# One turning transfer for the two chunks of a group, and a new order of loads and preparations, in a retention-and-mixer kernel

## The chip, the cores and the metric

The kernel runs on 1 core of one Trainium2 chip. The metric is the time of one execution in microseconds on the device; the profile is of one such execution. The engines of the core are named as in the profile: PE is TensorE (PEld its weight loads), DVE VectorE, ACT ScalarE, POOL GpSimd, SP SyncE. All loads from memory and all turning transfers (DMAs that transpose 16-bit data within the on-chip memory) are issued by SP, in the order of its queue; weights and most results go out by POOL's queue.

## The reference

```python
# q, k, v: (8 batches, 8 heads, 576 rows, 64), float32
scores = scale * q @ k.T                      # per batch and head
Dmat   = gamma[h] ** (i - j) for i >= j, else 0
x      = ((scores * Dmat) @ v)  -> (batch, 576, 512)      # heads side by side
h      = x.T @ U @ V                          # U: (576, 32), V: (32, 576)
u      = x + h.T
out    = u + max(u @ w_ch1, 0) @ w_ch2        # w_ch1: (512, 2048), w_ch2: (2048, 512)
```

## The kernel before

**Tiling.** Two batches lie one behind the other as 1152 rows, cut into nine chunks of 128 rows (`NI = 9`); the fifth chunk of a pair (`J = 4`) holds the last 64 rows of one batch and the first 64 of the next, so that it is loaded in halves. The first pair of batches is worked on by a front that is written out by hand (`front`, L937 to L1182). The three other pairs are the stream: 27 chunks, numbered 0 to 26 here, where chunk n is `order[NI + n]`.

**One streamed chunk.** `load` (L245) issues on SP the DMAs of k, q and v into three float32 tiles of the pool `stage` (15 tiles; L257). `prep` (L616) then does three things: `cast_qk` (L262) makes bf16 of k (L271, on VectorE for the first chunks, on POOL from chunk 5 on) and of q (L273, on ACT); `scale_v` (L277) makes bf16 of v times a decay (L282, POOL); `xbar` (L287) issues on SP one turning transfer of the chunk's q and k, 128x1024 elements (L290). The turned tile `qkT` feeds the scores, the bf16 k and v the states.

**Groups.** The stream is worked on in groups of one or two chunks: 0 | 1,2 | 3,4 | 5 | 6,7 | 8, and then twice (two, two, one, two, two): 9,10 | 11,12 | 13 | 14,15 | 16,17 and so on (L1194). Four steps belong to a group: W swaps halves of v (`swap_v`, L364, VectorE); S is `section` (L428): the output products of the group before (L401, L412), the scores of this one (L321, which need `qkT`), its state products (L338), and on VectorE the scaling of the outputs (L420) and the running states (L371, L373); C casts the states on ACT (L380); M multiplies the scores by the mask on VectorE (L351).

**The body.** For each batch b from 1 to 7 (L1233) a list of large products is the main work: `Y1` (L545), u times w_ch1 into one of three PSUM buffers (L553), evicted with a maximum on ACT (L559); `Y2` (L583), the result times w_ch2 (L588), to which VectorE adds u (L577) and which POOL stores (L580). Into this list `merge` (L16) puts the other steps, each at a share of the list's estimated cost that is written out by hand: `fills` (L1223) has W, S, C and M and the mixer's steps, `places` (L1215) the shares at which chunks are loaded and prepared. The mixer of the next batch (`mixer_items`, L441) makes u: two small products (L457, L493), an addition on VectorE (L499), and the turning of u on SP (L511), four chunks in one transfer of 128x2048 for an even batch, three and two chunks for an odd one. Each engine runs its instructions in the order in which they are written out so, and SP too: a transfer that waits for a cast holds back every load behind it.

Of the kernel before, what the change touches and what calls it, by code (L numbers as in the profile page):

```python
# [10 lines left out]
BF16 = mybir.dt.bfloat16  # L11
# [25 lines left out]
def kernel(  # L37
# [11 lines left out]
    nc = tc.nc  # L49

    B, H, S, D = q.shape
    dm = H * D
    dff = moe_w_ch1.shape[1]
    R = moe_U.shape[1]
    P = 128
    HALF = 64
    NHP = H // 2
    NF = dff // P
    NCC = dm // P
    NI = 9  # L60
# [7 lines left out]
    def pool(name, bufs, **kw):  # L68
        return ctx.enter_context(tc.tile_pool(name=name, bufs=bufs, **kw))

    consts = pool("consts", 1)
    stage = pool("stage", 15)
    qk_pool = pool("qk_pool", 9)
    v_pool = pool("v_pool", 9)
    qkT_pool = pool("qkT_pool", 9)
    ret_pool = pool("ret_pool", 5)
    s_pool = pool("s_pool", 2)
    x_pool = pool("x_pool", 1)
# [162 lines left out]
        return [(slice(0, HALF), e, J * P), (slice(HALF, P), e + 1, 0)]  # L241

    ch = {}

    def load(pr, i, which, seg=None, gate=False):  # L245
        c = ch.setdefault((pr, i), {})
# [15 lines left out]
    def cast_qk(pr, i, rows=slice(0, P), eng=None, k_eng=None, js=(1, 0)):  # L262
        c = ch[pr, i]
        if "qk" not in c:
            c["qk"] = qk_pool.tile([P, 2, dm], BF16, tag="qk", name="qk")
        t = c["qk"]
        if eng is not None:
            for j in js:
                copy(eng, t[rows, j, :], c["f", j][rows].rearrange("p h d -> p (h d)"))
            return  # L270
        (k_eng or nc.vector).tensor_copy(  # L271
            out=t[rows, 1, :], in_=c["f", 1][rows].rearrange("p h d -> p (h d)"))
        nc.scalar.activation(  # L273
            out=t[rows, 0, :], in_=c["f", 0][rows].rearrange("p h d -> p (h d)"),
            func=AF.Copy)
# [9 lines left out]
        )  # L285

    def xbar(pr, i):  # L287
        c = ch[pr, i]
        c["qkT"] = qkT_pool.tile([P, 2 * NHP, P], BF16, tag="qkT", name="qkT")
        nc.sync.dma_start_transpose(  # L290
            out=c["qkT"], in_=c["qk"].rearrange("p j n -> p (j n)")
        )

    st = {}

# [318 lines left out]
    order = [(pr, i) for pr in range(B // 2) for i in range(NI)]  # L614

    def prep(g):  # L616
        pr, i = order[g]
        cast_qk(pr, i, k_eng=nc.gpsimd if g >= NI + 5 else None)
        scale_v(pr, i)
        xbar(pr, i)  # L620

    un = [dict() for _ in range(4)]
    def unit_i0(u):
        return 2 * u + (1 if u >= 2 else 0)

    def unit_views(u, j, hh):
        if j not in un[u]:
            un[u][j] = qk_pool.tile([P, 2, dm], BF16, tag="qk", name="qk")
        w = slice(hh * 4 * D, (hh + 1) * 4 * D)
        return (un[u][j][:, :, w].rearrange("p j (h d) -> p h j d", d=D),  # L630
                un[u]["f", j, hh].rearrange("p (h j) d -> p h j d", j=2))
# [24 lines left out]
    def T_cp(u, j, eng, hps=slice(0, NHP)):  # L656
        pst = un[u]["pst", j]
        if ("T", j) not in un[u]:
            un[u]["T", j] = qkT_pool.tile([P, 2 * NHP, P], BF16, tag="qkT", name="qkT")
        t = un[u]["T", j]  # L660
        if j == 1:
            copy(eng, t, pst)
            return

        copy(eng, t.rearrange("p a b -> p (a b)").rearrange(
            "p (hp t j) -> p j hp t", hp=NHP, j=2)[:, :, hps],
            pst.rearrange("p (j hp) t -> p j hp t", j=2)[:, :, hps])
# [110 lines left out]
    def cast_J(r, eng, js):  # L778
        c = ch[0, J]
        if "qk" not in c:  # L780
            c["qk"] = qk_pool.tile([P, 2, dm], BF16, tag="qk", name="qk")
        for j in js:
            copy(eng, c["qk"][r, j, :].rearrange("p (t h d) -> p h t d", t=2, d=D),
                 c["f", j][r].rearrange("p (h t) d -> p h t d", t=2))
# [11 lines left out]
    def T_J(r, engs, k_at=None, q_at=None):  # L796
        c = ch[0, J]
        pst = {}
        for j, (pool_, tag) in ((1, k_at or (ps_big, "big")), (0, q_at or (ps_big, "big"))):
            pst[j] = pool_.tile([P, NHP, P], BF16, tag=tag, name="pst")  # L800
            for x in range(2):
                for t in range(2):
                    nc.tensor.transpose(  # L803
                        pst[j][:, 2 * x + t, r], c["qk"][r, j, (2 * t + x) * P:(2 * t + x + 1) * P],
                        ident[r, r])
        if "qkT" not in c:
            c["qkT"] = qkT_pool.tile([P, 2 * NHP, P], BF16, tag="qkT", name="qkT")
            c["kT"] = kTJ
        copy(engs[0], c["kT"][:, :, r], pst[1][:, :, r])
        o = c["qkT"][:, 0:NHP, r].rearrange("p (g x) (n t) -> p x t g n", g=2, t=2)  # L810
        i_ = pst[0][:, :, r].rearrange("p (x t) (g n) -> p x t g n", t=2, g=2)
        for x in range(2):
            copy(engs[1], o[:, x], i_[:, x])
# [106 lines left out]
    def gated_w2(f, block):  # L920

        nc.gpsimd.tensor_copy(
            out=gate[0:1, 0:1], in_=st["y1", 1][0:1, block, P:P + 1])
        load_w2(f)
# [259 lines left out]
    with tc.manual_schedule():  # L1184
        early_consts()
        y1_left = front()

        def placed(loads, preps):
            return ([(p, lambda g=g: load(*order[g], (1, 0, 2))) for g, p in loads]
                    + [(p, lambda g=g: prep(g)) for g, p in preps])  # L1190

        stream = [(pr, i) for pr in range(1, B // 2) for i in range(NI)]
        groups, n = [], 0
        for size in (1, 2, 2, 1, 2, 1) + 2 * (2, 2, 1, 2, 2):  # L1194
            groups.append(stream[n:n + size])
            n += size

        done = {"S": 0, "C": 0, "M": 0, "W": 0}
        scores = {}

        def step(kind):
            n = done[kind]
            done[kind] += 1
            new = groups[n] if n < len(groups) else []
            if kind == "S":
                scores[n] = section(new, groups[n - 1] if n else [])
            elif kind == "C":
                cast_states(new)
            elif kind == "M":
                mask(new, scores[n])  # L1210
            else:
                for c in new:
                    swap_v(*c)

        places = {  # L1215
            1: ((0.11, 0.24, 0.41, 0.53, 0.70, 0.85),
                (0.06, 0.20, 0.32, 0.47, 0.60, 0.69, 0.90)),
            2: ((0.02, 0.14, 0.30, 0.55, 0.75), (0.05, 0.22, 0.40, 0.58, 0.85)),
            3: ((0.02, 0.16, 0.32, 0.60, 0.85), (0.06, 0.23, 0.40, 0.56)),
            4: ((0.15, 0.32, 0.50, 0.80), (0.05, 0.20, 0.42, 0.62, 0.88)),  # L1220
            5: ((0.02, 0.16, 0.32), (0.06, 0.23, 0.40, 0.56)),
        }
        fills = {  # L1223
            1: ("W.19 S.22 C.24 M.24 W.34 S.42 C.44 M.45 W.50 S.58 C.60 M.61 "
                "W.68 S.71 C.73 M.76 W.86 S.95 C.97 M1", (0.75, 0.79)),
            2: ("W.22 S.25 C.28 M.27 W.42 S.52 C.55 M.75 W.82 S.90 C.94 M1", (0.58, 0.64, 0.70)),
            3: ("W.20 S.25 C.28 M.27 W.45 S.52 C.54 M.71 W.80 S.90 C.94 M1", (0.58, 0.65)),
            4: ("W.42 S.52 C.55 M.75 W.82 S.90 C.94 M1", (0.58, 0.64, 0.70)),
            5: ("W.20 S.25 C.28 M.27 W.45 S.52 C.54 M.71 W.80 S.90 C.94 M1", (0.58, 0.65)),
            6: ("S.20", (0.33, 0.40, 0.47)),  # L1230
        }
        gl, gp = NI + 4, NI + 2
        for b in range(1, B):  # L1233
            pr, par = divmod(b, 2)
            fill = []
            main = y1_items(par) + y2_items(pr, par)
            if b == 1:
                main = y1_left + y2_items(0, 0) + y2_items(0, 1)
            if b + 1 < B:
                steps, at_m = fills[b]  # L1240
                fill += [(float(w[1:]), lambda k=w[0]: step(k)) for w in steps.split()]
                mix = mixer_items((b + 1) // 2, (b + 1) % 2)[:-1]
                assert len(at_m) == len(mix)
                fill += list(zip(at_m, mix))
                if b == 1:
                    fill += [(p, lambda f=f, n=n: gated_w2(f, n))
                             for p, f, n in ((0.05, 12, 6), (0.11, 14, 8))]
            at_l, at_p = places.get(b, ((), ()))
            aux = placed(list(zip(range(gl, gl + len(at_l)), at_l)),
                         list(zip(range(gp, gp + len(at_p)), at_p)))  # L1250
            gl, gp = gl + len(at_l), gp + len(at_p)
            merge(main, fill, aux)
        assert done["S"] == len(groups) + 1
        assert gl == len(order) and gp == len(order)
# [29 lines left out]
```

## Time and profile before

| | |
|---|---|
| median of 3 runs | 317.97 us (317.72 to 319.87) |
| the profiled execution | 318.2 us, span of its instructions 316.4 us |
| PE busy | 307.7 us, 97% of the span |
| VectorE, ACT, POOL busy | 170.0, 135.8, 92.0 us |
| DMA queue of SP | 40.40 MB, 62.3% of the engines' time |
| granted TensorE clock | 1.00 |
| turns of q and k (L290) | 27, 2.7 to 9.1 us from issue to landing, median 4.4 |
| turns of u (L511) | 9, 3.1 to 7.8 us, median 4.6 |

The profile gives for each engine its busy time, for each wait the engine that waited and what ended the wait, and for each DMA the time of its issue on a queue (SPq, POOLq) and the time to landing. The chain that ended last is followed backwards from the last instruction, each time to what released it.

### The profile page before, as it was taken

The numbers are of one execution on the slowest core, as the hardware profiler recorded it, in microseconds if no ns is written. First come the engines' busy times: TensorE is split into PE (matmuls) and PEld (weight loads), VectorE is DVE, ScalarE is ACT, GpSimd is POOL, SyncE is SP. The second block draws the span as 40 slices with busy tenths as digits, with TensorE's granted clock in tenths as the row PEclk, the third lists the DMA queues.
The fourth block names the chain that finished last, engine by engine and source line by source line (L and its number), as shares of the span: only waits on it lengthen the run. The fifth ranks groups of instructions, "written<-read, shape, count | busy, mean of one in ns | idle before, by whom it ended". The sixth has DMA issues, their size and how long they took to land.

```text
span 316.4 us, 9217 instructions
## 1 busy us (share of the span) xinstructions
PE 307.7 (97%) x3962; PEld 168.2 (53%) x3962; DVE 170.0 (54%) x334; ACT 135.8 (43%) x285; POOL 92.0 (29%) x142
## 2 busy tenths in 40 slices
PE   8899999999979999999999999999999999999995
PEld 3565554554534444467654445467645444467544
DVE  7872667337977753993258714892368614100012
ACT  3747558752120475147820474147720463057300
POOL 6755925313422424143311430352301100200000
PEclk9999999999999999999999999999999999999999
DMA  7999899999999999999929596999635105110021
GB/s 218 258 236 258 202 216 217 208 193 223 213 202 231 251 234 181 210 227 235 205 71 239 160 217 150 201 223 248 151 55 147 68 2 85 66 67 2 0 99 69
DMA packets 149881, 53.31 MB, mean 169 GB/s; under 512 B 129008, under 2 KB 147312, under 8 KB 149840
## 3 DMA queue, kind: packets, MB, share of 16 engines
q1 hardware_dynamic: 143072, 40.40, 62.3%
q0 software_dynamic: 6768, 12.32, 15.9%
q8 instruction: 31, 0.51, 0.7%
q14 instruction: 10, 0.08, 0.1%
HBM read 36.85 MB, written 9.44 MB: 146 GB/s over the span
## 4 chain that ended last, share of the span: by engine, by line
PE 75%; DMA 11%; SPq 5%; DVE 3%; issue 2%; POOL 2%; ACT 1%; POOLq 0%; DVEq 0%; ACTq 0%
PE ps_y L553 35%; PE ps_y L588 30%; DMA stage_t<-in_k_dram 3%; DMA stage_t<-in_v_dram 3%; DMA qkT<-qk 3%; SPq L931 2%; DMA stage_t<-in_q_dram 2%; SPq L257 1%; PE po L401 1%; PE ph L493 1%; PE ps_y L599 1%; PE psc L321 1%; PE po L412 1%; PE pa L457 1%; PE inc L338 1%
## 5 line engine op out<-in xcount | busy, mean ns | idle before, releaser
L553 PE MATMUL ps_y<-uT,w 128*128 128x512 bf16 (+3 forms) x768 | 130.3, 326 | 0.1
L588 PE MATMUL ps_y<-w_sb,y 128*128 128x512 bf16 x560 | 126.2, 379 | 0.0
L559 ACT ACTIVATE y<-ps_y 128x384 bf16<-128x384 f32 (+2 forms) x192 | 89.0, 490 | 49.7 <-PE ps_y L553 48.7
L553 PEld LDWEIGHTS <-w 128*128 128x128 bf16 x768 | 71.2, 98 | 51.2 <-issue 1.6
L588 PEld LDWEIGHTS <-y 128*128 128x128 bf16 x560 | 52.6, 98 | 61.2
L577 DVE TENSOR_TENSOR o_sb<-ps_y,u 128x512 f32<-128x512 f32 (+2 forms) x38 | 25.1, 661 | 55.8 <-PE ps_y L588 53.4
L580 POOL DMA_DIRECT2D out_dram<-o_sb x31 | 17.4, 561 | 107.1 <-DVE o_sb L577 96.2
L380 ACT ACTIVATE s_sb<-s_f 128x1024 bf16<-128x1024 f32 (+1 forms) x16 | 14.7, 921 | 73.7 <-DVE s_f L373 64.4
L420 DVE TENSOR_TENSOR xt<-po,qscale 128x512 bf16<-128x512 f32 x27 | 17.6, 685 | 44.9 <-PE po L412 44.8
L282 POOL TENSOR_TENSOR vt<-stage_t,vscale 128x512 bf16<-128x512 f32 x27 | 28.2, 1044 | 39.7 <-DMA stage_t<-in_v_dram 33.8
L351 DVE TENSOR_TENSOR ret<-psc,tri 64x512 bf16<-64x512 f32 (+1 forms) x64 | 38.6, 603 | 1.2
L499 DVE TENSOR_TENSOR u<-ph,xt 128x512 bf16<-128x512 f32 (+4 forms) x33 | 22.4, 733 | 13.5 <-PE ph L493 13.5
L273 ACT ACTIVATE qk<-stage_t 128x512 bf16<-128x512 f32 x27 | 16.9, 624 | 23.2 <-DMA stage_t<-in_q_dram 23.2
L271 POOL CAST qk<-stage_t 128x512 bf16<-128x512 f32 x22 | 13.5, 615 | 25.1 <-DMA stage_t<-in_k_dram 19.3
L373 DVE TENSOR_TENSOR s_f<-inc,s_f 128x256 f32<-128x256 f32 x38 | 16.1, 423 | 1.6
L364 DVE COPY vs<-vt 64x256 bf16<-64x256 bf16 x54 | 15.4, 286 | 1.0
L638 POOL CAST qk<-stage_t 128x512 bf16<-128x512 f32 x16 | 9.7, 616 | 3.5 <-DMA stage_t<-in_q_dram 1.8
L218 PE MATMUL pw<-ident 128*128 128x512 bf16 x27 | 9.1, 473 | 1.4 <-POOL ident masks.py:199 1.4
L690 DVE TENSOR_TENSOR ret<-psc,triU 128x1024 bf16<-128x1024 f32 x8 | 9.5, 1220 | 1.3 <-PE psc L682 1.1
L750 DVE COPY qkT<-pst 128x1024 bf16<-128x1024 bf16 (+2 forms) x10 | 5.8, 603 | 5.9 <-PE pst L803 3.5
L321 PE MATMUL psc<-qkT 64*64 64x64 bf16 x432 | 7.1, 196 | 1.8 <-DMA qkT<-qk 1.8
L642 POOL TENSOR_TENSOR qk<-stage_t,vscaleU 128x512 bf16<-128x512 f32 x7 | 7.3, 1060 | 3.3 <-DMA stage_t<-in_v_dram 3.2
(116 smaller groups left out, 176.8 us busy)
## 6 DMA issues: line engine op xcount, KB each, us to landing
stage_t<-in_k_dram SPq DMA_DIRECT2D x32, 256.0 KB, 4.2
stage_t<-in_q_dram SPq DMA_DIRECT2D x32, 256.0 KB, 4.9
stage_t<-in_v_dram SPq DMA_DIRECT2D x32, 256.0 KB, 5.3
out_dram<-o_sb POOLq DMA_DIRECT2D x31, 256.0 KB, 3.7
w<-in_moe_w_ch_dram POOLq DMA_DIRECT2D x4, 512.0 KB, 8.3
w_sb<-in_moe_w_ch_dram POOLq DMA_DIRECT2D x8, 256.0 KB, 6.6
out_dram<-o_sb SPq DMA_DIRECT2D x4, 256.0 KB, 2.0
stage_t<-in_k_dram SPq DMA_DIRECT2D x6, 128.0 KB, 3.9
```

What stands on the lines that cost most here:

```text
L273: nc.scalar.activation(out=t[rows, 0, :], in_=c["f", 0][rows].rearrange("p h d -> p (h d)"), func=AF.Copy)
L282: (eng or nc.gpsimd).tensor_tensor(out=c["v"][rows], in0=c["f", 2][rows], in1=vscale[rows, i, :, None].to_broadcast([n, H, D]), op=ALU.mult,)
L351: nc.vector.tensor_tensor(out=ret[o, n, 0:m], in0=psc[t, hl, 0:m * D].rearrange("p (b i) -> p b i", i=D), in1=tri[t, None, t].to_broadcast ...
L364: nc.vector.tensor_copy(out=c["vs"][o], in_=v[HALVES[1 - hl], hl])
L373: nc.vector.tensor_tensor(out=s_f[:, s, :], in0=src, in1=s_f[:, st["f_end"], :], op=ALU.add)
L420: nc.vector.tensor_tensor(out=x_of(pr, i).rearrange("p (hp hl d) -> p hl hp d", hl=2, d=D), in0=po[:, :, a * SW:(a + 1) * SW].rearrange("p ...
L499: nc.vector.tensor_tensor(out=st["u", par][:, i0 - base:i0 - base + n, w].rearrange("p s (c d) -> p c s d", c=len(ccs)), in0=t[:, :, 0:n, ...
L553: nc.tensor.matmul(ps[:, 0:n, :], w1_t[f * P // W1B][:, cc, f * P % W1B:f * P % W1B + P], st["uT", par][:, c0:c0 + n, cc, :], start=(cc == ...
L559: nc.scalar.activation(out=st["y1", par][:, f, c0 * P:(c0 + n) * P], in_=ps[:, 0:n, :].rearrange("p s t -> p (s t)"), func=AF.Relu)
L577: nc.vector.tensor_tensor(out=o_sb[:, 0:n], in0=ps[:, 0:n], in1=st["u", par][:, c, w], op=ALU.add)
L580: (nc.sync if last else nc.gpsimd).dma_start(out=out_flat[r0:r0 + P, w], in_=o_sb[:, 0:n])
L588: nc.tensor.matmul(ps, st["y1", par][:, f, c * P:(c + 1) * P], w2_sb[:, f, :], start=(f == 0), stop=(f == NF - 1),)
```

## The change

The two chunks of a group share one tile for the bf16 q and k and one for the turned ones; the turning transfer is issued once for both, at the preparation of the second, as 128x2048. Groups of one chunk (but for 8) use a tile of their own with a single buffer. Pools that held 9 tiles of one chunk hold 4 tiles of two. In the front the tiles of a unit (256 rows, `unit_views`, `T_cp`) are put together in the same way. The q of chunks 9, 10 and 11 is cast by POOL and not by ACT. In batch 1 loads 5, 6, 7 and 9 are issued later, preparation 5 a little earlier, and v of chunk 8 is loaded apart, behind the turning of u of batch 2. In batch 2 loads 10, 11, 12 come later, preparations 9, 10, 11 later, and preparation 12 earlier, ahead of load 13. Batches 3 to 7 keep their places.

```diff
-    qk_pool = pool("qk_pool", 9)
+    qk_pool = pool("qk_pool", 4)
-    qkT_pool = pool("qkT_pool", 9)
+    qkT_pool = pool("qkT_pool", 4)
...
+    sizes = (1, 2, 2, 1, 2, 1) + 2 * (2, 2, 1, 2, 2)
+    mates, n_ch = {}, NI
+    for n_g, size in enumerate(sizes):
+        for a in range(size):
+            mates[n_ch + a] = (n_g, a, size)
+        n_ch += size
+    turn = {}
+
+    def group(pr, i):
+        n, a, size = mates[pr * NI + i]
+        if n not in turn:
+            alone = size == 1 and n != 5
+            turn[n] = (qk_pool.tile([P, 1, 2, dm], BF16, tag="qk1", bufs=1, name="qk") if alone
+                       else qk_pool.tile([P, 2, 2, dm], BF16, tag="qk", name="qk"))
+        return turn[n], n, a, size
...
     def xbar(pr, i):
-        c = ch[pr, i]
-        c["qkT"] = qkT_pool.tile([P, 2 * NHP, P], BF16, tag="qkT", name="qkT")
+        pair, n, a, size = group(pr, i)
+        if a < size - 1:
+            return
+        alone = size == 1 and n != 5
+        t = (qkT_pool.tile([P, 2 * NHP, P], BF16, tag="qkT1", bufs=1, name="qkT") if alone
+             else qkT_pool.tile([P, 4 * NHP, P], BF16, tag="qkT", name="qkT"))
         nc.sync.dma_start_transpose(
-            out=c["qkT"], in_=c["qk"].rearrange("p j n -> p (j n)")
+            out=t[:, 0:2 * NHP * size, :],
+            in_=pair[:, 0:size].rearrange("p a j n -> p (a j n)")
         )
...
     def prep(g):
         pr, i = order[g]
-        cast_qk(pr, i, k_eng=nc.gpsimd if g >= NI + 5 else None)
+        cast_qk(pr, i, eng=nc.gpsimd if NI + 9 <= g <= NI + 11 else None,
+                k_eng=nc.gpsimd if g >= NI + 5 else None)
...
         def placed(loads, preps):
-            return ([(p, lambda g=g: load(*order[g], (1, 0, 2))) for g, p in loads]
+            return ([(p, lambda g=g: load(*order[g], (1, 0) if g == split_load else (1, 0, 2)))
+                     for g, p in loads]
                     + [(p, lambda g=g: prep(g)) for g, p in preps])
 
+        split_load = NI + 8
...
-            1: ((0.11, 0.24, 0.41, 0.53, 0.70, 0.85),
-                (0.06, 0.20, 0.32, 0.47, 0.60, 0.69, 0.90)),
-            2: ((0.02, 0.14, 0.30, 0.55, 0.75), (0.05, 0.22, 0.40, 0.58, 0.85)),
+            1: ((0.11, 0.31, 0.47, 0.55, 0.70, 0.93),
+                (0.06, 0.20, 0.30, 0.46, 0.60, 0.69, 0.90)),
+            2: ((0.10, 0.27, 0.42, 0.55, 0.75), (0.14, 0.26, 0.45, 0.54, 0.85)),
...
+                    fill.append((0.83, lambda: load(*order[split_load], (2,))))
```

In `places` the first list of a batch is the loads (in batch 1 of chunks 4 to 9, in batch 2 of 10 to 14), the second the preparations (2 to 8, and 9 to 13).

## The prediction

> **What bounds the kernel now.** I read the page first: busy shares, then the chain that ended last.
>
> ```profile
> PE 307.7 (97%) x3962; PEld 168.2 (53%) x3962; DVE 170.0 (54%) x334; ACT 135.8 (43%) x285; POOL 92.0 (29%) x142
> ...
> PE 75%; DMA 11%; SPq 5%; DVE 3%; issue 2%; POOL 2%; ACT 1%; POOLq 0%; DVEq 0%; ACTq 0%
> ```
>
> TensorE is busy for 307.7 of 316.4 us, at a granted clock of 1.0 throughout. The change alters no TensorE instruction, so it can win only idle time: 8.7 us in all. Next the table by stages and TensorE's waits, to see where that lies.
>
> ```profile
> 56.70:106.00 49.30, 47.52 (x684) 24.32 (x682) 31.84 (x68) 14.82 (x32) 15.95 (x23) 1.00 1.13 217
> 106.00:138.60 32.60, 32.60 (x477) 15.77 (x476) 21.78 (x47) 14.42 (x25) 10.50 (x14) 1.00 1.07 219
> ```
>
> ```profile
> PE psc L321 <- DMA qkT<-qk: 1.8, 1, 1.8
> PE pw L218 <- POOL ident masks.py:199: 1.4, 1, 1.4
> ```
>
> From 56.7 us (the code of batch 1) to 249 us TensorE idles once (but for 0.05 at 211): 1.78 us (49.30 - 47.52; the first columns of a row are the stretch, its length and TensorE's busy time) at L321, the scores of a group, until a turning transfer lands. The rest is the front (3.7 us before 56.7) and the end (3.2 us after 249), whose order stays. So 1.78 us is the whole prize. The chain around it and the SP queue show why the transfer is late.
>
> ```profile
> 82.88 8.56 DMA qkT<-qk
> 91.43 0.04 issue
> 91.48 0.32 PE psc L321 x16
> ```
>
> ```profile
> 77.94 2.30 SPq L290 DMA_TRANSPOSE qkT<-qk  x1
> 80.30 0.57 SPq L257 DMA_DIRECT2D stage_t<-in_k_dram  x1
> 80.92 0.58 SPq L257 DMA_DIRECT2D stage_t<-in_q_dram  x1
> 81.54 1.23 SPq L257 DMA_DIRECT2D stage_t<-in_v_dram  x1
> 82.88 3.81 SPq L290 DMA_TRANSPOSE qkT<-qk  x1
> ```
>
> I number the streamed chunks 0 to 26; groups are 0 | 1,2 | 3,4 | 5 | 6,7 | 8 | 9,10 | 11,12 | 13 | 14,15 and so on. Chunk 5's turn is issued at 82.88 behind the three loads of chunk 6 and needs 8.6 us. Without the wait TensorE would be there at 91.48 - 1.78 = 89.70. In the chain, later groups start their scores at 103.70, 113.86, 122.47 and 135.46; the turns before them landed at 99.1 (94.30 + 4.8), 111.7 (105.54 + 6.2), 121.4 (115.97 + 5.4) and 133.4 (129.94 + 3.5). Once TensorE is 1.78 us earlier, the third would be 0.7 us late, unless the queue gets faster too.
>
> **Paired turns.** 27 transfers become 16: 11 pairs and 5 singles. A pair is 128x2048, the shape that u's turn over four chunks already has; two rows of the trace price it and the single:
>
> ```profile
> L290 SPq DMA_TRANSPOSE qkT<-qk x27: 1231/1934/4511, 52.0 to 233.8; - x27
> DMA to landing us min/median/max: 2.7/4.4/9.1
> ```
>
> ```profile
> L511 SPq DMA_TRANSPOSE uT<-u x9: 1233/1418/3894, 98.9 to 266.0; - x9
> DMA to landing us min/median/max: 3.1/4.6/7.8
> ```
>
> The three 2048-wide ones at L511 took 3.82, 3.89 and 1.64 us to issue and 5.8, 7.8 and 4.3 us to land, so I bound a pair by 4.3 and 7.8 us. On SP the change takes away 11 issues of 1.93 us and lengthens 11 others by -0.3 to 2.0 us (1.64 and 3.89 against 1.93): 24.5 to -0.3 us less, off TensorE's path except where named below. In the queue a turn costs more than a load: the chunk after the turn issued at 111.51 (landed 115.5) was issued at 113.53 and landed at 118.5, 3.0 us behind it, while loads follow each other 0.9 to 1.0 us apart (80.30 + 3.5, 80.92 + 3.8). Two turns fewer per two pairs should therefore shorten the queue. The Trainium skill, Advanced Engine Details and Errata, section X-Bar Transpose (TRN2), states that turning transfers are as fast as plain ones; by that, pairing frees no queue time at all. This trace's 3.0 us speaks against it, and a rival below takes the case.
>
> Buffers: pairs in rings of 4 and singles in one buffer make waits coarser, but in the order of the changed kernel each such wait is for work long done (unit 3's cast waits for unit 1's state products, which end at 18.9; the cast ran at 34.2). Zero.
>
> **Chunk 5 (the prize).** The pair 3,4 needs chunk 4's q cast, ACT 72.96 + 0.63 = 73.6; SP is through chunk 4's loads at 71.9, so the issue is at 73.6. It lands at 77.9 to 81.4, against 82.3 (77.94 + 4.4) for chunk 4 before and a need at 83.0. Chunk 5's loads follow at 75.3 to 77.5 instead of 73.43; q, 0.6 to 1.1 us later, needs 3.8 to 5.2 us and lands at about 80 to 83.8; its cast (0.62; ACT's previous work ended at 78.8) makes the turn ready at 80.7 to 84.4. POOL now runs chunk 4's v cast (1.03 us from 74.34) ahead of two stores (0.62, 0.60), so it is free at 76.6, ahead of chunk 5's k: zero. The turn has no load of chunk 6 ahead of it any more. I take 82.5 + 4.4 (the median of singles, nearest since SP stands still before it and the queue drains) = 86.9, 2.8 us before the need. Gain 1.78 us. Bounds: 80.7 + 2.7 is early; 84.4 + 9.1 = 93.5 leaves 3.8 us of wait, 2.0 more than now.
>
> **Chunks 6 to 10.** Pair 6,7 waits for POOL's k cast of 7 behind a store whose o_sb ends at 89.5: issue about 91, landed by 98.8, need 103.70 - 1.78 = 101.9. u of batch 2 is ready at 98.77 - 1.78 = 97.0; its turn moves ahead of chunk 8's v and lands 4.3 to 7.8 later, by 104.8; needed at 106.14 - 1.78 = 104.4. I take 5.8, its own row: no wait; bound 0.4. Three q casts (0.62 each) go from ACT to POOL (0.61 as for k). POOL's run for 9 and 10 is 4 x 0.61 + 2 x 1.04 = 4.5 us, beside landings about 1 us apart, so the pair is issued near 111.5 and lands by 119.3; need 122.47 - 1.78 = 120.7. Zero.
>
> The Trainium skill, SBUF — State Buffer, section Who interferes with whom, holds that VectorE and GpSimd can lock one port pair against each other for a whole instruction. The trace has such a case: the copies at L364 took 1.78 us for four at 81.13 beside POOL's L282, against 0.93 at 71.85. By it, three casts would cost VectorE up to 1.9 us around 107 to 122, where it waits 3.9 and 4.3 us for L412; that hides it.
>
> **Chunk 12 and batch 3's start (what is late next).** Chunk 12's q cast stays on ACT behind the state cast L380 of group 9,10 (125.34 + 1.06 = 126.4): 1.78 earlier, it ends at 125.2. SP now stands at the pair 11,12 from about 117 until 125.3, with chunk 13's six half loads, u's two turns and chunk 14's loads behind it; before, the half loads had left from 123.86. The pair itself lands at 129.6 to 133.1; need 135.46 - 1.78 = 133.7: zero. Then 1.64 us of issue, six half loads at 4.5 us (67.33 to 71.85) to 5.9 us (123.86 to 129.77), two turns 3.2 us: chunk 14's k leaves at 134.6 to 136.0, against 134.57 before, though TensorE is 1.78 us earlier. Two needs follow. The second turn leaves about 132.9 and with its former 4.3 us lands at 137.2; Y1 needs it one 128x384 product (0.65) after its start, 138.77 - 1.78 + 0.65 = 137.6: just in time. And ACT holds chunk 14's q cast after the fourth y; before, q landed at 140.6 (135.21 + 5.4) and was cast at 141.41. ACT gets there at 139.6. Y1 has three PSUM buffers: the fifth y ended at 142.3 (141.92 + 0.38), and the eighth product, which needs that buffer, began at 138.60 + 4 x 0.65 + 3 x 0.43 = 142.5. So TensorE tolerates 0.2 us more: 139.8. Landing: 135.3 + 4.9 (the median of q loads) = 140.2; bounds 135.2 + 3.5 = 138.7 (quietest row) and 136.6 + 5.4 = 142.0. Loss 0.4, bounds 0 and 2.2; with the turn's tight case I take 0.5.
>
> Batches 4 to 7 keep their places; their turns landed 3.1 to 7 us ahead of their scores, and a pair costs at most 3.4 us more than the median single (7.8 - 4.4): zero, 0.3 at the bound.
>
> **Sum.** The profiled execution took 318.2 us (1.8 around the span of 316.4); 318.2 - 1.78 + 0.5 = 316.9. It stood 0.2 above the median 317.97, so the median comes to 316.7.
>
> **Rivals.**
> 1. Nothing is given back: chunk 14's q lands by 139.8, as in the quiet rows. 318.0 - 1.8 = 316.2. For it: the queue has drained while SP stood still. Against: its six half loads now leave in one go behind a pair.
> 2. Slower: SP's stand at pair 11,12 makes u's second turn late. With L511's longest 7.8 us it lands at 140.7 and Y1 waits 3.1 us: 318.0 - 1.78 + 3.1 = 319.3. It decides from a landing after 137.6 + 1.8 = 139.4. Against: L511's median is 4.6, and no chunk's turn stands right ahead of it any more.
> 3. The gap stays: chunk 5's turn again takes long (its bound lands at 93.5). A landing at 91.4 gives no change, 318.0. Against: no loads are ahead of it.
> 4. Pairing frees no queue time: chunk 10's turn lands at 121.4 as before, against 120.7: the wait moves there, 0.7 us, 318.0 - 1.8 + 0.7 = 316.9 before batch 3's loss, about 317.4 with it. Against: the 3.0 us row. The section X-Bar Transpose (TRN2) of the Trainium skill would have it so.
>
> **How the numbers follow.** Forecast 40%, rival 1 28%, rival 2 12%, rival 3 8%, rival 4 7%, others 5%. The forecast's own range is 316.2 to 317.9 (0 to 1.7 of the loss). The whole range, 315.8 to 319.3, takes in all four rivals, with 0.4 us of spread below the first, and leaves out the others. About 1% (3.2 us) is what a measurement of this kernel can tell from no change. Every case but rival 2's far end lies within it, since the prize itself is 0.6%: faster by over 1% 3%, within 1% 90%, slower by over 1% 7%.
>
> **What would show it.** Right: no wait at L321 for a turn near 90; 16 turns of q and k; chunk 5's turn landing near 87; SP waiting at the pair 11,12 for ACT's L273 until about 125; a TensorE wait of some tenths at L553 near 137 to 140, ended by ACT or u's turn; idle in the body below 1.2 us. Wrong: the wait at L321 still there or moved to a later group; idle before L553 above 1.8 us; a longer front.

## The result: 0.7% slower

Over 19 runs of each kernel the changed one takes 319.78 us (318.81 to 323.15), the kernel before 317.82 us (316.21 to 319.87): a ratio of 1.0068, 95% interval 1.0043 to 1.0092, so about 2.2 us slower. A second comparison of the same two kernels (12 and 35 runs) gave 1.0024 (0.9991 to 1.0057), an interval that takes in no change. The ratios leave out executions more than 1.5% above the fastest of their kernel; in e3 these are seven of twelve and in e16 four, the profiled ones among them, so that these two profiles are read for single waits and stretches alone. The forecast was 1.3 us faster (316.7); its range of 315.8 to 319.3 ends 0.5 us below the measured time.

The profiled execution took 320.5 us, with a span of 318.7 (before 318.2 and 316.4). First the page of the changed kernel: busy time of the engines, and the shares of the chain that ended last.

```profile
PE 307.9 (97%) x3962; PEld 168.0 (53%) x3962; DVE 168.8 (53%) x334; ACT 135.0 (42%) x282; POOL 93.3 (29%) x145
...
PE 68%; DMA 15%; SPq 6%; DVE 4%; issue 2%; POOL 2%; ACT 2%; POOLq 0%; ACTq 0%; DVEq 0%
```

TensorE's work is as long as before (307.7); what grew is its idle time, and the DMA's share of the chain rose from 11% to 15%. The same stages as in the prediction, and one more (stretch, its length, TensorE's busy time first); the last line is that stage in the kernel before:

```profile
56.70:106.00 49.30, 46.82 (x679) 24.11 (x678) 30.44 (x66) 14.93 (x32) 14.83 (x22) 1.00 1.08 209
106.00:138.60 32.60, 32.40 (x478) 15.78 (x476) 22.10 (x47) 13.22 (x22) 12.40 (x18) 1.00 1.07 212
138.60:170.00 31.40, 30.80 (x388) 18.94 (x387) 15.78 (x33) 17.64 (x40) 8.97 (x12) 1.00 0.85 180
138.60:170.00 31.40, 31.40 (x392) 19.42 (x391) 17.37 (x33) 17.28 (x40) 8.40 (x11) 1.00 0.87 181
```

Before, only the first of the three had idle time, 1.78 us. Now they have 2.48, 0.20 and 0.60. TensorE's waits in the changed kernel (us in total, times, the longest) name them:

```profile
PE ps_y L576 <- ACT y L582: 1.5, 1, 1.5
...
PE ph L516 <- ACT a_sb L488: 1.2, 2, 1.0
...
PE ps_y L576 <- DMA uT<-u: 0.4, 1, 0.4
```

The wait for chunk 5's turn at the scores (L321 before, L344 now) is gone. In its place stand four others: 1.52 at 69.08 (evictions on ACT behind the cast of chunk 2's q), 0.95 at 96.88 and 0.21 at 128.08 (both L516, the mixer), and 0.38 + 0.22 at 140.2 to 141.3, the start of Y1 in batch 3. (The 0.22 is put down to VectorE's L374 by the profile, but u's second turn landed only at 141.12, and the product that began at 141.26 is the first that needs it.) The timeline of SP shows where the last ones come from:

```profile
123.39 1.24 SPq L272 DMA_DIRECT2D stage_t<-in_v_dram  x1
127.93 1.56 SPq L310 DMA_TRANSPOSE qkT<-qk  x1
129.53 1.34 SPq L272 DMA_DIRECT2D stage_t<-in_k_dram  x2
130.92 1.40 SPq L272 DMA_DIRECT2D stage_t<-in_q_dram  x2
132.37 1.31 SPq L272 DMA_DIRECT2D stage_t<-in_v_dram  x2
133.78 3.90 SPq L534 DMA_TRANSPOSE uT<-u  x2
137.73 0.58 SPq L272 DMA_DIRECT2D stage_t<-in_k_dram  x1
```

SP stands from 124.7 to 127.9 at the turn of chunks 11 and 12. Then come six half loads of chunk 13, and only then u's two turns, at 133.78 and 136.38, which land at 140.17 and 141.12. VectorE had the first part of u ready at 130.4 (128.51 + 1.89), 3.4 us before its turn was issued. In the kernel before, the half loads stood ahead of chunk 12's turn, and SP did not stand there (L290 and L257 there are L310 and L272 here, L511 is L534):

```profile
123.86 1.32 SPq L257 DMA_DIRECT2D stage_t<-in_k_dram  x2
125.22 3.04 SPq L257 DMA_DIRECT2D stage_t<-in_q_dram  x2
128.30 1.47 SPq L257 DMA_DIRECT2D stage_t<-in_v_dram  x2
129.94 1.31 SPq L290 DMA_TRANSPOSE qkT<-qk  x1
131.35 3.17 SPq L511 DMA_TRANSPOSE uT<-u  x2
```

### The profile page after: what moved, and what is told of

It reads as the page before. It is cut to its first block, busy times and chain, and to the rows that moved or that the text cites. A ratio compares the mean times of both kernels' runs of the same rounds, so it can differ in the third digit from the quotient of the medians.

```text
span 318.7 us, 9154 instructions
## 1 busy us (share of the span) xinstructions
PE 307.9 (97%) x3962; PEld 168.0 (53%) x3962; DVE 168.8 (53%) x334; ACT 135.0 (42%) x282; POOL 93.3 (29%) x145
## 4 chain that ended last, share of the span: by engine, by line
PE 68%; DMA 15%; SPq 6%; DVE 4%; issue 2%; POOL 2%; ACT 2%; POOLq 0%; ACTq 0%; DVEq 0%
PE ps_y L576 32%; PE ps_y L611 28%; DMA stage_t<-in_q_dram 9%; DMA stage_t<-in_v_dram 4%; SPq L272 2%; SPq L310 2%; DMA stage_t<-in_k_dram 1%; PE po L424 1%; PE ph L516 1%; PE ps_y L622 1%; SPq L962 1%; SPq L803 1%; DVE s_f L396 1%; PE po L435 1%; PE psc L344 1%
## 5 line engine op out<-in xcount | busy, mean ns | idle before, releaser
L374 DVE TENSOR_TENSOR ret<-psc,tri 64x512 bf16<-64x512 f32 (+1 forms) x64 | 38.6, 603 | 1.2
L289 ACT ACTIVATE qk<-stage_t 128x512 bf16<-128x512 f32 x24 | 14.9, 624 | 29.4 <-DMA stage_t<-in_q_dram 29.4
L287 POOL CAST qk<-stage_t 128x512 bf16<-128x512 f32 x19 | 11.7, 615 | 20.0 <-DMA stage_t<-in_k_dram 18.9
L387 DVE COPY vs<-vt 64x256 bf16<-64x256 bf16 x54 | 14.5, 268 | 1.5 <-POOL vt L298 0.6
L667 POOL CAST qk<-stage_t 128x512 bf16<-128x512 f32 x16 | 9.7, 617 | 3.3 <-DMA stage_t<-in_q_dram 1.8
L781 POOL CAST qk<-stage_t 128x512 bf16<-128x512 f32 (+1 forms) x9 | 5.5, 612 | 9.6 <-DMA stage_t<-in_k_dram 4.0
L779 ACT ACTIVATE s_sb<-pss 64x256 bf16<-64x256 f32 (+1 forms) x18 | 6.4, 355 | 4.5 <-PE pss L770 4.2
```

The costliest lines, as they stand in the source:

```text
L289: nc.scalar.activation(out=t[rows, 0, :], in_=c["f", 0][rows].rearrange("p h d -> p (h d)"), func=AF.Copy)
L374: nc.vector.tensor_tensor(out=ret[o, n, 0:m], in0=psc[t, hl, 0:m * D].rearrange("p (b i) -> p b i", i=D), in1=tri[t, None, t].to_broadcast ...
```

## Experiments

To compare profiles without the front, I use the body: from the start of the scores of chunk 0 to the start of the scores of the last group. It is 178.56 us in the kernel before (66.00 to 244.56) and 180.57 in the changed one (66.14 to 246.71). Some profiles have up to 13 stops of TensorE of 0.16 us before products of Y2, which end on nothing that the profile shows; they are left out where waits are counted.

**e4 and e8: the two kernels once more, unchanged, for a second profile.**

> The changed kernel once more, for a second profile. Theories A and B: a wait near 69 us for ACT of 0.7 to 2 us again, and 0.9 near 97. Theory C: no wait near 69, a time 1.5 us shorter, near 317 for the profiled execution's span.

> The kernel before once more, for a second profile. If the wait of 1.78 us for chunk 5's turn is there in every execution, it shows again near 91 (1 to 2.5 us); if it was chance, it is under 0.5 us, and the pairs alone had nothing to win, as their time says.

e4 (320.27 us) has no wait at 69; of the eighteen profiles here only the first of the changed kernel and e16's have it, so it belongs to some executions only. At the mixer it waits 0.42 and 0.20, at Y1 of batch 3 0.91 and 0.79 for u's turns; body 179.75. e8 (316.94 us) has no wait at L321: chunk 5's turn was issued at 82.09, the same place in the queue, and landed at 88.84, before the need. Its body is 176.49 us, 2.07 shorter than in the first profile. So the 1.78 us that were to be won belong to some executions only.

**e1 and e11: the pairs alone.** Everything but the pairing is as before; against the changed kernel, without the lines of the split load (the first lists show that in batch 1 the change also issues preparation 4 a little earlier, at 0.30 and not 0.32):

```
-        cast_qk(pr, i, eng=nc.gpsimd if NI + 9 <= g <= NI + 11 else None,
-                k_eng=nc.gpsimd if g >= NI + 5 else None)
+        cast_qk(pr, i, k_eng=nc.gpsimd if g >= NI + 5 else None)
...
-            1: ((0.11, 0.31, 0.47, 0.55, 0.70, 0.93),
-                (0.06, 0.20, 0.30, 0.46, 0.60, 0.69, 0.90)),
-            2: ((0.10, 0.27, 0.42, 0.55, 0.75), (0.14, 0.26, 0.45, 0.54, 0.85)),
+            1: ((0.11, 0.24, 0.41, 0.53, 0.70, 0.85),
+                (0.06, 0.20, 0.32, 0.47, 0.60, 0.69, 0.90)),
+            2: ((0.02, 0.14, 0.30, 0.55, 0.75), (0.05, 0.22, 0.40, 0.58, 0.85)),
```

> The kernel before with the pairing alone: loads, preparations and the engines of the q casts as before. Theory A (TensorE loses time where a cast of q in ACT's queue waits for a load and holds back an eviction; the shifted loads 7 and 12 cause 0.95 + 0.2 us of it, u's later turns 0.6, the front and chunk 2 the 1.5 us at 69): a wait for ACT near 69 of up to 1.5 us, none at the mixer of 97 us, about 317.5 to 319.0. Theory B (the wider turns themselves hold up the queue and cost the 2 us): about 319.8, as the changed kernel, with q landing late behind pairs also in batches 3 to 7. Theory C (the wait at 69 is chance of the profiled execution, the loss is in the shifts): 316.5 to 318, and no wait at 69.

> The kernel of e1 once more (the pairs alone, everything else as before), to narrow its interval. Theory A: no wait on TensorE above 0.2 us between 57 and 249 us, at or under the kernel before by up to 0.8 us. Theory B (the wide turns cost time themselves): 0.5 us or more above it.

Ratio to the kernel before 0.9991 (0.9963 to 1.0019) and 0.9995 (0.9959 to 1.0031). e1 has no wait in the body above 0.12 (body 177.14); e11 waits 1.54 for u's turn of batch 2 near 105 (178.69). By these times the wide turns cost nothing that shows, and win nothing that shows: theory B fell.

**e2: the shifts alone**, with one turn for each chunk; the diff is the change without its pool and tile edits.

> The changed places, the split load and the q casts on POOL, but one turn for each chunk as before. Theory A: the waits at the mixer of batch 2 (about 97 us, for ACT behind chunk 7's q, 0.9 us) and at Y1 of batch 3 (0.4 to 0.6) stay, a wait near 69 does not depend on this edit: 318.5 to 320. Theory B: without the wider turns no loss, 316 to 318. Theory C: 319 to 320 with no wait near 69.

1.0015 (0.9983 to 1.0047), which is not clear of the kernel before; its profile has the waits of theory A, 1.62 at the mixer, 0.51 and 0.50 at Y1 of batch 3, body 179.42. The two waits come with the shifts, not with the pairs.

**e3: three casts moved to POOL.**

```
         cast_qk(pr, i, eng=nc.gpsimd if NI + 9 <= g <= NI + 11 else None,
-                k_eng=nc.gpsimd if g >= NI + 5 else None)
+                k_eng=nc.gpsimd if g >= NI + 5 else None,
+                q_pool=g - NI in (2, 7, 12))
```

> The changed kernel, with q of chunks 2, 7 and 12 cast by POOL instead of ACT, so that no eviction and no copy of the mixer stands behind these three late loads. Theory A: the waits of 1.52 us near 69, 0.95 near 97 and 0.2 near 128 go: 319.8 - 2.7 = 317.1 (316.7 to 317.9). Theory B: the turns still come late, the wait only changes its name (scores wait for the turn): 319 to 320. Theory C: only the 0.95 and the 0.2 go, 318.6.

A miss: 1.0064 (1.0015 to 1.0112). The waits at 69, at the mixer of batch 2 and at 128 are gone, as expected, but Y1 of batch 3 now waits 2.58 us for u. Chunk 12's q landed at 128.78 and the pair's turn left at 129.47, 1.5 later than in the changed kernel, and u's second turn followed at 137.59 (136.38 there). Here the load of q itself, 6.29 us on its way, held SP at that turn, and the cast on POOL could not help.

**e6, e5, e7 and e10: preparation 12 back behind load 13; batch 1 back; both, twice.** e6 has the first edit, e5 the second (and chunk 8's v loaded with its k and q again), e7 and e10 have both.

```
-            2: ((0.10, 0.27, 0.42, 0.55, 0.75), (0.14, 0.26, 0.45, 0.54, 0.85)),
+            2: ((0.10, 0.27, 0.42, 0.55, 0.75), (0.14, 0.26, 0.45, 0.58, 0.85)),
...
-            1: ((0.11, 0.31, 0.47, 0.55, 0.70, 0.93),
-                (0.06, 0.20, 0.30, 0.46, 0.60, 0.69, 0.90)),
+            1: ((0.11, 0.24, 0.41, 0.53, 0.70, 0.85),
+                (0.06, 0.20, 0.32, 0.47, 0.60, 0.69, 0.90)),
```

> The changed kernel with preparation 12 back at 0.58, so that chunk 13's six half loads are issued ahead of the turn of 11 and 12 while SP would stand, and ACT copies the mixer's sums ahead of chunk 12's q. Theory A: u's second turn lands at 136 to 138, the wait at Y1 near 140 goes (0.6 to 1.7 us) and the 0.2 near 128 too; the one at 95 to 97 stays: 319.8 - 1.2 = 318.6 (318.0 to 319.2). Rival D: the turn of 11 and 12 now lands late, the wait moves to the scores near 135, 319.5 to 320.5.

> The changed kernel with the loads and preparations of batch 1 (4 to 9) in their old places and chunk 8's v not loaded apart; batch 2 and the pairs stay as changed. Theory A (two places lose the time: batch 1's later loads bring chunk 7's q late, its cast stands in ACT's queue ahead of the mixer's copy, 0.4 to 1.6 us at L516 near 95 to 97; and preparation 12 ahead of load 13 brings u's turns for batch 3 late, 0.6 to 1.7 us at Y1 near 140): the first goes, the second stays or grows by what TensorE comes earlier: 318.5 to 319.5. Rival D (the queue as a whole is too slow, and time taken out at one place comes back at the next): the wait at Y1 grows by all that is won, 319.8 as the changed kernel.

> Both at once: batch 1's old places without the split load, and preparation 12 at 0.58; left of the change are the pairs, POOL's q casts and the later places of batch 2. Theory A: no wait on TensorE between 57 and 249 us above 0.2, 316.8 to 317.8, as the pairs alone. Rival D: a wait of 1 us or more for a transfer in batch 2 or 3, 318.5 to 320.

> The kernel of e7 once more (pairs, POOL's q casts, later places of batch 2, preparation 12 back at 0.58, batch 1 as before), to narrow its interval. Theory A: no wait on TensorE above 0.2 us between 57 and 249 us; 0 to 0.8 us under the kernel before, which waits for chunk 5's turn in some of its executions only. Rival D: a wait of 1 us or more for a transfer again, 0.5 us or more above the kernel before.

e6: 0.9974 (0.9941 to 1.0006), 317.92 us and so below theory A's 318.0 to 319.2. No wait at Y1; 0.61 at the mixer; 0.36 at the scores of 11 and 12 near 135. e5: 1.0051 (1.0014 to 1.0088); it waits at Y1 of batch 3 (0.24) and also for chunk 5's turn (0.77) and u of batch 2 (0.68); its time does not tell theory A from rival D. e7: 0.9974 (0.9936 to 1.0012), no wait above 0.12 in the body, 176.77; the same kernel as e10: 0.9984 (0.9950 to 1.0018), one wait of 1.16 at the scores of 11 and 12, whose turn took 8.8 us to land. So rival D holds in one of these two executions: with the half loads ahead, the pair's turn can come late instead. SP in e6, for comparison with the fence above:

```profile
122.52 1.54 SPq L272 DMA_DIRECT2D stage_t<-in_k_dram  x2
124.11 2.80 SPq L272 DMA_DIRECT2D stage_t<-in_q_dram  x2
126.95 1.31 SPq L272 DMA_DIRECT2D stage_t<-in_v_dram  x2
128.43 3.37 SPq L310 DMA_TRANSPOSE qkT<-qk  x1
131.90 2.87 SPq L534 DMA_TRANSPOSE uT<-u  x2
```

The half loads now fill the time in which SP stood, and u's turns follow the pair at once.

**e9: preparation 12 alone, in the kernel before.**

```
-            2: ((0.02, 0.14, 0.30, 0.55, 0.75), (0.05, 0.22, 0.40, 0.58, 0.85)),
+            2: ((0.02, 0.14, 0.30, 0.55, 0.75), (0.05, 0.22, 0.40, 0.54, 0.85)),
```

> The kernel before with one number changed: preparation 12 at 0.54 instead of 0.58, ahead of load 13, and nothing else of the change. Theory A (this step alone makes the loss): SP stands at chunk 12's turn until ACT has cast its q, near 127, the six half loads leave after it, u's two turns 2 to 4 us later than before, landing at 138 to 141, and Y1 of batch 3 waits 0.5 to 2.5 us for them near 139: 1 to 2 us slower than before, 319 to 320. Rival E (the loss needs the later loads 10 to 12 of the change, or the pairs, too): no wait above 0.3 at Y1 there, 317.5 to 318.3.

1.0038 (1.0002 to 1.0074): 1.2 us slower by the ratio, near the low end of theory A's range. SP stood 3.15 us at chunk 12's turn, u's turns left at 132.30 and 135.19 and landed at 138.63 and 139.31, and Y1 began at 138.68, 0.05 us after the first of them landed, as in every profile in which it waits for u; but TensorE had only just finished its work before, so no wait of theory A's 0.5 to 2.5 us shows there. The loss shows when the profile is read from a point that moves with TensorE, the scores of 9 and 10: from there to the scores of chunk 13 this kernel takes 26.47 us (122.19 to 148.66), where the kernel before takes 25.80 (122.30 to 148.10), as it does in every profile in which nothing waits. Of these 0.7 us, 0.19 are Y1's later start and 0.37 a wait at 143.23 for an eviction behind chunk 14's q (landed 142.10). Rival E's "no wait above 0.3 at Y1" holds, but there is a loss without the later loads and without the pairs. Earlier in the same execution TensorE waited for chunk 5's turn at 91.00,

```profile
PE psc L321 <- DMA qkT<-qk: 1.7, 1, 1.7
```

and 0.40 for u's turn of batch 2 at 106.07; both places lie ahead of the edited one in the program.

**e12: batch 2 back, batch 1 as changed.** The q casts are on ACT again, and

```
-            2: ((0.10, 0.27, 0.42, 0.55, 0.75), (0.14, 0.26, 0.45, 0.54, 0.85)),
+            2: ((0.02, 0.14, 0.30, 0.55, 0.75), (0.05, 0.22, 0.40, 0.58, 0.85)),
```

> The pairs and batch 1 as in the changed kernel, batch 2 (places and engines of the q casts) as before. Theory A: the wait of 0.4 to 1.6 us at the mixer of batch 2 near 95 to 97 for ACT behind chunk 7's q stays, none at Y1 of batch 3 near 140; it costs what TensorE doesn't stand at a later place anyway: 0 to 1 us above the kernel before. Rival F (the places of batch 1 carry as much of the loss as preparation 12): 1.5 to 2.2 us above it.

1.0097 (1.0059 to 1.0135), more than the change itself and than theory A or rival F expected, but for a reason of its own: load 9 is at 0.93 of batch 1 as in the change, preparation 9 at 0.05 of batch 2 as before. ACT stood for chunk 9's q with two evictions behind it:

```profile
106.49 1.11 ACT L582 ACTIVATE y<-ps_y 128x512 bf16<-128x512 f32 x2
110.65 0.63 ACT L289 ACTIVATE qk<-stage_t 128x512 bf16<-128x512 f32 x1 [3.05 <-DMA stage_t<-in_q_dram]
111.19 1.07 ACT L582 ACTIVATE y<-ps_y 128x512 bf16<-128x512 f32 x2
```

TensorE waited 2.26 us for them. So this mixture says nothing of batch 1's weight.

**e13 to e16: the weight of the parts, on one chip.** e13 is the changed kernel unchanged. e14 and e15 move preparation 7 behind the mixer's copy, as below; e14 and e16 have preparation 12 at 0.58; e16 is e2 otherwise.

```
-                (0.06, 0.20, 0.30, 0.46, 0.60, 0.69, 0.90)),
+                (0.06, 0.20, 0.30, 0.46, 0.60, 0.755, 0.90)),
```

> The changed kernel once more, beside the next three. All theories: 1 to 3 us above the kernel before; Y1 of batch 3 waits 0.6 to 1.7 us for u's turns near 140, the mixer of batch 2 0.4 to 1.0 us for ACT near 95 to 97.

> The changed kernel with preparation 7 at 0.755, behind the mixer's copy on ACT and behind chunk 8's k and q on SP, and preparation 12 at 0.58. Theory A: neither the wait at the mixer near 95 to 97 nor the one at Y1 near 140 is there: 2 us or more under e13, 0 to 1 us under the kernel before. Rival F (the loss lies elsewhere in the shifts or in the wide turns): 1 us or more above the kernel before.

> The changed kernel with preparation 7 alone moved to 0.755; preparation 12 stays ahead of load 13. Theory A (preparation 12 carries most): the wait at the mixer goes, that at Y1 of batch 3 stays or grows to 1 to 2.5 us: 0 to 0.8 us under e13. Rival F (batch 1's part is the larger): 1.2 us or more under e13.

> One turn for each chunk as before, all shifts of the change but preparation 12, which is at 0.58. Theory A (without preparation 12's early place the shifts cost only the mixer's wait): no wait at Y1 near 140, within 0.7 us of the kernel before. Rival G (the pairs are needed for the shifts to work): a wait for a single turn of 1 us or more at the scores near 103, 113 or 122, 1 us or more above it.

e13: 1.0024 (0.9991 to 1.0057), 0.8 us and so under the 1 to 3 expected; its wait at Y1 0.43, and 0.48 more behind chunk 14's q; no wait at the mixer near 97, which was expected. e15: 1.0054 (1.0018 to 1.0089); the mixer's wait is gone, and u's turns cost 0.62 + 0.35, the copy behind chunk 12's q 0.56. e14: 1.0014 (0.9979 to 1.0048), no wait in the body above 0.12 (176.81). e16: 0.9969 (0.9929 to 1.0009); its profile waits 2.34 at 70 behind chunk 2's q and 0.61 for chunk 12's turn, and not at Y1; without a wait of 1 us for a single turn, rival G fell. e14's time is less good than its profile; by its interval it can't be told from the kernel before. Rival F fell: without batch 1's wait the loss stays.

**All together.** Five pairs of kernels differ in one number alone, preparation 12 at 0.54 or 0.58. Ratios to the kernel before, each from its own comparison with it:

| the rest of the kernel | 0.54 | 0.58 | difference |
|---|---|---|---|
| as changed | 1.0068, 1.0024 | 0.9974 (e6) | 0.7% |
| as changed, batch 1 as before | 1.0051 (e5) | 0.9974 (e7), 0.9984 (e10) | 0.7% |
| as changed, preparation 7 later | 1.0054 (e15) | 1.0014 (e14) | 0.4% |
| as changed, single turns | 1.0015 (e2) | 0.9969 (e16) | 0.5% |
| as before | 1.0038 (e9) | 1 | 0.4% |

All five have the same sign, their mean is 0.54%, 1.7 us (equal runs averaged); taken as independent, the intervals of the ratios make that about 0.2% either way (an estimate). With every execution counted, the means of the runs give 0.63, 0.54, 0.55, 0.01 and 0.21%, on average 0.39% or 1.2 us: the three rows with pairs stand, the two with single turns are weak. So the loss by this one place is 1.2 to 1.7 us.

The profiles agree. From the scores of 9 and 10 to those of chunk 13 they take 25.8 us where nothing waits. With 0.54 it is 26.5 to 28.3 in seven executions, mean 27.2 (30.1 in e3); with 0.58 it is 25.8 to 27.1 in nine, mean 26.0 (26.5 in e16). Y1 of batch 3 waits 0.2 to 2.6 us for u's turns in seven of the eight executions with 0.54 (in e9 no idle time shows), and at most 0.16 us in the ten with 0.58. In the seven with 0.54 whose landing is recorded, Y1 begins 0.05 us after the first turn lands, in e9 too.

None of the kernels with 0.58 but e12 is clear of the kernel before; e6 and e7 are clearly faster only than the changed kernel in its first comparison.

## Why the prediction was wrong, point by point

Two terms of the sum were mis-sized: the gain at chunk 5, and the loss at chunk 12 and the start of batch 3. The kernels with the new places of batch 1 and preparation 12 at 0.58 (e6, e14, e16; e12 aside, with its own wait) come to 0.9986 on average, a gain of about 0.4 us and not 1.78; preparation 12's place costs 1.2 to 1.7 us and not 0.5. With these two the forecast's sum is 318.0 - 0.4 + 1.2 to 1.7 = 318.8 to 319.3 (an estimate); measured were 319.78, and 0.8 us above the kernel before in the second comparison.

- **The prize (step "Chunk 5").** The mechanism was right: with the new places no load of chunk 6 stands ahead, and chunk 5's turn, forecast for 82.5 and 86.9, was issued at 84.25 and landed at 88.61. None of the ten profiles with these places waits for it. It is the places that do this and not the pair: e1, e5, e7, e10 and e11 have pairs and the old places, and e5 still waits 0.77. The size was wrong. 1.78 us were taken from one execution as if they were in each; of three profiles of this code (the first, e8, and e9, which differs only further on) two have the wait and one has none, and e6, e14 and e16, which take it away, lie between -0.3% and +0.1% of the kernel before. The forecast needed the wait's frequency, and one profile doesn't give it.
- **Chunks 6 to 10, "no wait".** This step failed as well. It tied the pair 6 and 7 to POOL ("issue about 91"; it was issued at 96.20) and left out what stands behind its other half: chunk 7's q, whose load now follows SP's stand of 2.67 us at chunk 5's turn. It landed at 95.49, and the mixer's copy L488 stood behind the cast in ACT's queue. The chain near 97 us, in order of time:

```profile
90.47 5.02 DMA stage_t<-in_q_dram
95.49 0.02 issue
95.51 0.04 ACT qk L289
95.56 0.49 issue
96.05 0.61 ACT s_sb L403
96.66 0.17 ACT a_sb L488
96.84 0.04 issue
96.88 0.41 PE ph L516 x16
```

  It costs 0.95, 0.42 and 0 us in three profiles of the changed kernel. Whether that reaches the end is another matter: e15 takes it away and is no faster. The Trainium skill, PSUM — Partial Sum Buffer, section Engine vs sequencer instructions, says that the queue of ScalarE is strictly first in, first out; this chain and e12's 2.26 us agree.

  Two more of this step's zeros came out by a narrow margin or by luck. The pair 9 and 10, forecast to be issued near 111.5 and to land by 119.3, was issued at 117.26 and landed at 120.89, after the need of 120.7 that the prediction had worked out; nothing waited because TensorE itself came at 123.03. And u's turn for batch 2 took 6.95 us and not 5.8, landing at 106.72, 0.23 before Y1 began.
- **Chunk 12 and batch 3's start.** The place was right: SP stands for ACT's cast, the half loads leave behind it, and u's turns and chunk 14 come late. The pair was issued 4.9 us after the scores of its forerunner began (127.93 - 123.03), as forecast (125.3 - 120.5 = 4.8). What failed is "just in time", and with it the loss of 0.5: from the scores of 9 and 10 to those of 13 the three profiles of the changed kernel take 26.89, 27.37 and 28.26 us, 1.1 to 2.5 more than before. The second turn was priced by its row of before (1.65 to issue, 4.3 to land) and left at 13.4 us after those scores instead of 12.4, since the first took 2.50 to issue and not 1.42; the two took 6.39 and 4.75 to land, where the rows of before were 4.98 and 4.28. And the first turn's own need, 0.65 earlier, was not worked out at all. Rival 2 named this wait, with a chance of 12%; the slack of 0.4 us that it had against a row that varies between 3.1 and 7.8 deserved more. (It was 0.3: the starts that the prediction read from the chain lie 0.17 or 0.18 behind the first product in the timeline, 138.77 for 138.60, 122.47 for 122.30. No other step turns on that.) The mixer's copy behind chunk 12's q (0.2 to 0.56 at 128) was missed as well.
- **Chunk 14's q.** Forecast to land at 140.2 against a tolerance of 139.8, it landed at 143.25. In the changed kernel's first profile TensorE had already stood for u, and no wait came of it; in others 0.2 to 0.5 us did (0.48 in e13, 0.37 in e9, 0.20 in e4).
- **The pairs' price.** Bounded by 4.3 and 7.8 us to landing; the 11 pairs took 3.6 to 8.2, median 4.5, and the five single turns 4.4 to 9.4. The queue got no relief that shows in the times: rival 4's premise may hold, but no wait moved to group 9 and 10.
- **The sum.** Of the first two profiles' difference in the body, 2.01 us, the waits make 1.56: -1.78 for chunk 5, +1.52 at 69, which some executions have (e16, with single turns, has 2.34 there), +0.95 and +0.21 at the mixer, +0.60 at Y1, +0.06. 0.30 more lie in one stretch of Y1 (below). By times, preparation 12's place makes 1.2 to 1.7 us of the loss; the kernels of the table that keep the rest lie between -0.3% and +0.1%. Open is why e13 and the first comparison differ by 0.4% (their intervals overlap), and why e14's time is no better than its profile. The 1% that the prediction gave as what a measurement can tell from no change was too much: the interval of 19 runs each is 0.25% either way.

## What to carry to other kernels

A wait that one profile shows is not a cost of each execution: take a second profile before you count it as the prize, above all where a DMA's landing decides it. Before you move a transfer that waits for a cast ahead of transfers that wait for nothing, list everything behind it on that queue and what each of those may be late by; here six half loads could fill the wait, and in the new order they stood behind it. The same holds for a cast that waits for a load on an engine that also evicts.

## What was not expected of the hardware

- VectorE stops between the first and the second of the state additions at 206 to 214 us, waiting for nothing that the profile shows: 0.10 us in each of the five profiles with single turns, 0.45 to 0.47 us in each of the thirteen with pairs. In the changed kernel:

```profile
209.82 0.41 DVE L396 TENSOR_TENSOR s_f<-inc,s_f 128x256 f32<-128x256 f32 x1
210.69 1.34 DVE L396 TENSOR_TENSOR s_f<-inc,s_f 128x256 f32<-128x256 f32 x3 [0.45 <-DVE s_f L396]
```

  ACT's state cast and the evictions behind it follow later, and the stretch from the scores at 208.03 to those at 221.19 takes 13.16 us, where the kernel before needs 12.80 (206.24 to 219.04); 0.06 of it is a longer wait for ACT's `y`. It is 12.8 us in all five profiles with single turns and 13.2 in all thirteen with pairs, so that pairs carry some 0.36 us there. The cause was not tried.
- The first products of the front wait for the weights `w` near 42 us in some executions, whatever the kernel: 0.15 to 2.3 us in eleven of eighteen profiles. A single time of this kernel can't tell less than that.
